# Attention followed by two MLPs on one core: short attention matmul runs held back until a second one is ready

## The chip, the cores and the metric

One core of a Trainium2 chip runs the whole program. The metric is the device time of one execution in microseconds (us), as the median of several executions. The engines are TensorE (PE in the profile; PEld is its weight load), VectorE (DVE), ScalarE (ACT), GpSimd (POOL) and SyncE (SP), which issues every DMA.

## The reference

```python
def _attn_ref(q, k, v):                      # (4, 8, 576, 64)
    out_d = sm_attn(q_d, k_d, v_d)           # q, k, v averaged over 4 positions: 144
    out_up = np.repeat(out_d, factor, axis=2)
    mask = np.abs(pos[:, None] - pos[None, :]) < factor
    scores = np.where(mask, scale * np.matmul(q, k.transpose(0, 1, 3, 2)), -1e9)
    ...
    return out_up + np.matmul(attn, v)
def _moe_ref(x, w_in, w_out):                # 2304 x 512, 512 x 2048, 2048 x 512
    g = np.maximum(x @ w_in, 0.0) ** 2
    return g @ w_out
def reference(...):                          # attention, then two such MLPs
```

The attention of a batch is the sum of a coarse part (all heads over 144 averaged positions) and a local part (a band of seven positions around the diagonal). Its result, 2304 tokens of 512 numbers, goes through two MLPs of the same shape.

## The kernel before, in words

The MLPs work on nine tiles of 256 tokens. For each tile and each of eight slices p of the hidden layer, `mm_h` (L787) does 24 matmuls of 128 x 128 by 128 x 256, ACT squares the relu, and `mm_y` (L864) does 24 more. Weights and activations are split into a high part (wH, xH, gH) and a low part (xL, gL), each product being done in three. The first two tiles are interleaved slice by slice, since the weights are still being unpacked from 64 bits on ACT, DVE and POOL (L639, L641, L644, L653) in that time. I call these matmuls **F**: tiles 0 and 1 take F 1 to 768, and tile 2 begins at F 769.

The attention runs between them on TensorE, in short runs:

- `pool_qk` (three transposes, L383) and `pool_v` (POOL adds, L357 and L361, into vd) average q, k and v;
- `heads_of`, four times a batch: scores (L406), softmax, transposes of the probabilities (L433), product with the averaged values vd (L444), evacuation by ACT into outd;
- `group`, five times a batch, for 116 positions: transposes of q and k (L508), mask (L523) and scores (L532), softmax, transposes (L561), product with v (L579), and the sum with outd into the token tile xr (DVE, L591). ACT and POOL then split xr into xH (L329) and xL (L765) for the MLP.

The order of all of this is not written out. Each piece of work is a generator that yields what it needs next as an engine and an estimated duration; `Order.run` (L127 on) takes, again and again, the piece that could start earliest by its own estimate of time, and the instructions are issued in that order. So the order of all engines is fixed when the kernel is built, and each engine then runs its own list in sequence. The accumulators for the attention are whole PSUM tiles: at0 (at_138 in some listings), at1 and y. Once the MLP has begun, y and then at1 are given up to the MLP, so that until tile 1 has left, every attention run writes to at0 and waits until its last reader has finished.

`Order.fill` issues matmuls of no use while TensorE would be idle before the MLP begins (L990); it is unset at the MLP's first step.

Of the kernel before, what the change touches and what calls it, by code (L numbers as in the profile page):

```python
# [28 lines left out]
SAME = 0.03  # L29
TO_PE = 0.1  # L30
WINDOW = 10.24 / 3
COLS = 3300
NXL = 2
NXR = 2
# [7 lines left out]
NEAR = 0.02  # L42
# [7 lines left out]
class Thread:  # L50
    def __init__(self, gen, prio):
        self.gen, self.prio, self.ready, self.wish = gen, prio, 0.0, None
        self.last, self.done = None, 0.0


class Order:


    def __init__(self):
        self.free = {}  # L60
        self.columns = {}
        self.fill = None
        self.lanes = []
        self.live = []
        self.ev = {}

    def lane(self, width, todo):

        self.lanes.append((width, [Thread(g, p) for p, g in todo], []))
# [34 lines left out]
    def slow(self, t):  # L104

        return self.columns.get(int(t / WINDOW + 1e-9) - 1, 0.0) < COLS

    def stream(self, t, dur, rows=1.0):

        while dur > 1e-6:  # L110
            w = int(t / WINDOW + 1e-9)
            rate = 0.5 if self.slow(t) else 1.0
            part = min(dur, ((w + 1) * WINDOW - t) * rate)
            self.columns[w] = self.columns.get(w, 0.0) + part * 2400 * rows
            dur -= part
            t += part / rate
        return t

    def start(self, th, eng):
        own = 0.0 if eng == th.last == "SP" else th.done  # L120
        if eng != th.last:
            own += LATENCY.get(th.last, 0.0)
        elif eng not in ("PE", "SP"):
            own += SAME
        t = max(th.ready, own) + (TO_PE if eng == "PE" and th.last != "PE" else 0.0)
        t = max(t, self.free.get(eng, 0.0))
        return max(t, self.free.get("DMA", 0.0) - AHEAD) if eng == "SP" else t  # L127

    def run(self):
        while True:  # L130
            self.poll()
            best = None
            for th in self.live:
                if th.wish is not None and not callable(th.wish):
                    some = th.wish if isinstance(th.wish, list) else [th.wish]
                    _, t, eng, dur, *rows = min((self.start(th, w[0]) + w[1] * BIAS.get(w[0], 1.0), self.start(th, w[0]), *w) for w in some)
                    key = t
                    if best is None or key < best[0] - NEAR:
                        best = key, t, th, eng, dur, rows
            if best is None:  # L140
                assert not self.live, "nothing can start"
                return
            _, t, th, eng, dur, rows = best
            self.eng = eng
            if eng == "PE":
                if self.fill:
                    now = max(self.free.get("PE", 0.0), FT)
                    while now + FG < t:
                        now = self.stream(now, 0.22, 1.0)
                        self.fill()  # L150
                dur = self.stream(t, dur, *rows) - t
            if eng == "SP":
                self.free[eng] = t + (rows[0] if rows else 0.46)
                self.free["DMA"] = max(t + 1.1, self.free.get("DMA", 0.0)) + dur
                value = self.free["DMA"] + 2.0
            else:
                self.free[eng] = t + dur
                value = t + dur + LATENCY[eng]
            th.last, th.done = eng, value - LATENCY[eng]
            self.resume(th, value)  # L160
# [46 lines left out]
def attention_two_mlp_kernel(  # L207
# [101 lines left out]
    def dve(cols):  # L309
        return "DVE", 0.165 + cols / 960.0  # L310

    def dve2(cols):

        return "DVE", 0.2 + cols / 720.0
# [4 lines left out]
    def pool(cols):  # L319
        return "POOL", 0.12 + cols * 0.0026  # L320

    def act(cols):
        return "ACT", 0.185 + cols / 1200.0

    def engine():
        return nc.vector if o.eng == "DVE" else nc.gpsimd

    def evac(dst, src):
        nc.scalar.activation(out=dst, in_=src, func=AF.Copy)  # L329
# [5 lines left out]
    def count(key, n, t):  # L335

        c = counts.setdefault(key, [0, 0.0])
        c[0] += 1
        c[1] = max(c[1], t)
        if c[0] == n:  # L340
            ev[key] = c[1]
        return c[0] == n
# [51 lines left out]
    def heads_of(b, hp):  # L394

        yield o.at("pooled", b)
        m = yield from f_hd.take()
        pp, nm, sm = hd_[m], nm_[m][:, 0], nm_[m][:, 1]
        p4 = pp.rearrange("p (c g) -> p c g", c=4)
        a = yield from f_at.take()  # L400
        s = pair[a][0:72, :, 0:288].rearrange("p j (a g) -> p j a g", a=2)
        tt = yield "PE", 0.4
        for qh in range(2):
            for j in range(2):
                js = slice(64 * j, 64 * j + 64)
                nc.tensor.matmul(  # L406
                    out=s[:, j, qh], lhsT=qd[js, hp, 72 * qh:72 * qh + 72], rhs=kd[js, hp], start=True, stop=True
                )
        count(("scored", b), 4, tt)
        yield dve(576)  # L410
        nc.vector.tensor_reduce(out=nm.rearrange("p (j a) -> p j a", j=2), in_=s, op=ALU.max, axis=AX.X)
        yield "DVE", 0.2
        nc.vector.tensor_scalar_mul(nm, nm, -1.0 / 128.0)
        for c in range(4):
            tt = yield "ACT", 0.57
            nc.scalar.activation(
                out=p4[:, c], in_=s[:, c // 2, c % 2], func=AF.Exp, bias=nm[:, c:c + 1], scale=1.0 / 128.0,
                accum_out=sm[:, c:c + 1],
            )
        f_at.put(a, tt)  # L420
        yield "DVE", 0.2
        nc.vector.tensor_scalar(out=sm, in0=sm, scalar1=1e-9, scalar2=4.0, op0=ALU.add, op1=ALU.mult)
        yield "DVE", 0.2
        nc.vector.reciprocal(out=sm, in_=sm)
        yield [dve2(576), pool(576)]
        engine().tensor_tensor(out=p4, in0=p4, in1=sm.unsqueeze(2).to_broadcast([72, 4, GD]), op=ALU.mult)
        a = yield from f_at.take()
        yield "PE", 0.55, 0.56
        for j in range(2):
            for kh in range(2):  # L430
                for qh in range(2):
                    c = kh * 144 + qh * 72
                    nc.tensor.transpose(  # L433
                        pair[a][0:72, j, c:c + 72], p4[:, 2 * j + qh, kh * 72:kh * 72 + 72], ident[0:72, 0:72]
                    )
        yield act(576)
        evac(pp.rearrange("p (j c) -> p j c", j=2), pair[a][0:72, :, 0:288])
        yield o.at("vpooled", b)
        if b > 1:
            yield o.at("local", b - 2)  # L440
        tt = yield "PE", 0.5
        for kh in range(2):
            for j in range(2):
                nc.tensor.matmul(  # L444
                    out=pair[a][64 * j:64 * j + 64, 0, 288:432], lhsT=vd[:, 4 * j + hp, kh],
                    rhs=pp[:, j * 288 + kh * 144:j * 288 + kh * 144 + 144], start=(kh == 0), stop=(kh == 1),
                    skip_group_check=True,
                )
        count(("pved", b), 4, tt)
        tt = yield act(288)  # L450
        evac(
            outd[b % 2][:, 2 * (hp % 2) + hp // 2].rearrange("p (g r) -> p g r", r=2),
            pair[a][:, 0, 288:432].unsqueeze(2).to_broadcast([128, GD, 2]),
        )
        f_at.put(a, tt)
        f_hd.put(m, tt)
        count(("heads", b), 4, tt)
# [30 lines left out]
    def group(b, i):  # L488
# [16 lines left out]
        tt = yield "PE", 0.9  # L505
# [6 lines left out]
        tt = yield act(1024)  # L512
# [4 lines left out]
        u = yield from f_pb.take(b == 0)  # L517
        p, nm, sm = pb_[u], nmb_[u][:, 0], nmb_[u][:, 1]
        a = yield from f_at.take()
        yield "PE", 0.4  # L520
        mask = mask16[0 if i == 0 else 2 if i == NG - 1 else 1]
        for j in range(2):
            nc.tensor.matmul(  # L523
# [3 lines left out]
        tt = yield "PE", 0.5  # L527
# [15 lines left out]
        tt = yield dve(512)  # L543
# [18 lines left out]
        tt = yield act(512)  # L562
# [6 lines left out]
        t0, t1 = (b * S + q0) // TN, (b * S + q0 + nq - 1) // TN  # L569
        yield from x_tiles(t0, t1)  # L570
        a = yield from f_at.take()
        tt = yield "PE", 0.6
        xp = pair[a].rearrange("p j (i c) -> p (j i) c", i=2)
        for i2 in range(2):
            for c, qa, nb, w0 in blocks:
# [9 lines left out]
        for c, qa, nb, w0 in blocks:  # L585
            g = b * S + qa
            for t in range(g // TN, (g + nb - 1) // TN + 1):
                c0, c1 = max(g, t * TN), min(g + nb, t * TN + TN)
                o0, g0, n2 = 64 * c + c0 - g, (c0 - b * S) // 2, (c1 - c0) // 2
                tt = yield dve(4 * (c1 - c0))  # L590
# [369 lines left out]
    for b in range(B):  # L960
        t = b * S / TN - 2
        heads += [(t + QP, pool_qk(b, s_, d_, c)) for c in range(3) for s_, d_ in ((q, qd), (k, kd))]
        heads += [(t + VP, pool_v(b, kh, j)) for kh in range(2) for j in range(2)]
        heads += [(t + HP, heads_of(b, hp)) for hp in range(4)]
        vees += [((b * S + GQ * i) / TN + UP, values(b, i)) for i in range(NG)]
        groups += [((b * S + GQ * i) / TN + GP, group(b, i)) for i in range(NG)]
# [78 lines left out]
```

## Time and profile before

| what | us |
|---|---|
| median of three executions | 973.45 |
| lowest, highest | 972.92, 977.17 |
| profiled execution | 971.34 |
| its span, first to last instruction | 969.6 |
| TensorE busy in it | 930.5 (96%) |

TensorE is busy nearly all of the time from about 100 us on, and the attention's last run is over by about 408 us. The span is 1.7 us shorter than the time of its own execution, and that execution is 2.1 us below the median. "Idle before" in a row is time in which the engine stood still, and what stands behind the arrow is what ended it. The granted clock is given as a share of 2.4 GHz.

### The profile page before, as it was taken

What the parts mean: (1) busy time and instruction counts of PE and PEld (TensorE: products, weight loads), DVE (VectorE), ACT (ScalarE), POOL (GpSimd) and SP (SyncE); (2) the same over time, 40 slices, a digit from 0 to 9 for tenths busy, and PEclk for the clock granted to TensorE, in tenths of its full rate; (3) what the DMA queues carried; (4) which work ended last, traced back from release to release, by engine and by line L of the source; (5) the groups of instructions that cost most, each with busy time, mean ns of one, the idle gap of its engine ahead of it and who ended that gap; (6) DMA issues with size and microseconds to landing.
All of it is one profiled execution on the core that took longest, in us unless ns stands there. A gap on an engine that the chain in (4) does not pass through costs nothing.

```text
span 969.6 us, 21378 instructions
## 1 busy us (share of the span) xinstructions
PE 930.5 (96%) x8795; PEld 889.2 (92%) x8795; DVE 502.3 (52%) x1016; ACT 515.4 (53%) x1044; POOL 250.9 (26%) x236
## 2 busy tenths in 40 slices
PE   7877999999999999999999999999999999999996
PEld 4457888999999999999999999999999999999996
DVE  5599796333353666655311226545454554545454
ACT  4466666455565565544443656545455554545543
POOL 5265563236134200101653454201010110101000
PEclk9798999999999999999999999999999999999999
DMA  9676565146147466675230544011010101100000
GB/s 237 151 209 191 168 177 131 43 136 163 48 119 196 142 208 212 213 242 182 67 102 30 172 134 150 3 45 44 2 44 2 45 1 45 45 1 23 1 23 23
DMA packets 99538, 101.00 MB, mean 104 GB/s; under 512 B 66672, under 2 KB 72304, under 8 KB 99440
## 3 DMA queue, kind: packets, MB, share of 16 engines
q1 hardware_dynamic: 99440, 99.64, 34.8%
q8 instruction: 69, 1.13, 0.5%
q14 instruction: 29, 0.24, 0.1%
HBM read 80.74 MB, written 18.87 MB: 103 GB/s over the span
## 4 chain that ended last, share of the span: by engine, by line
PE 84%; DVE 6%; DMA 3%; ACT 3%; POOL 2%; issue 1%; SPq 1%; DVEq 0%; POOLq 0%; ACTq 0%
PE h L787 39%; PE y L864 17%; PE at L847 13%; PE y L847 5%; DVE ga L644 2%; PE at L864 2%; DMA ld<-in_moe_w_in_dram 2%; PE at L508 2%; PE at L532 1%; PE at L579 1%; DMA ld<-in_v_dram 1%; PE at L406 1%; PE h L990 1%; PE at L383 1%; PE at L561 1%
## 5 line engine op out<-in xcount | busy, mean ns | idle before, releaser
L787 PE MATMUL h<-xH,w 128*128 128x256 f32 x2304 | 325.1, 283 | 0.0
L787 PEld LDWEIGHTS h<-xH,w 128*128 128x128 f32 x2304 | 294.5, 190 | 2.2 <-issue 1.2
L796 ACT ACTIVATE h<-h 128x512 f32<-128x512 f32 x144 | 83.8, 582 | 199.6 <-PE h L787 199.5
L787 PE MATMUL h<-xL,w 128*128 128x256 f32 x1152 | 182.9, 280 | 0.0
L832 DVE TENSOR_TENSOR gL<-h,gH 128x512 fp32r<-128x512 f32 x144 | 98.6, 684 | 137.7 <-ACT gH L805 120.2
L787 PEld LDWEIGHTS h<-xL,w 128*128 128x128 f32 x1152 | 156.6, 189 | 0.0
L864 PE MATMUL y<-gH,w 128*128 128x256 f32 x1024 | 133.5, 283 | 2.9 <-ACT gH L805 2.9
L765 POOL TENSOR_TENSOR xL<-xr,xH 128x512 fp32r<-128x512 f32 x33 | 43.6, 1337 | 341.1 <-ACT xH L329 341.0
L828 DVE TENSOR_TENSOR S<-h,S 128x128 f32<-128x128 f32 x144 | 42.0, 291 | 169.5 <-ACT gH L805 165.3
L864 PEld LDWEIGHTS y<-gH,w 128*128 128x128 f32 x1024 | 125.6, 190 | 4.3 <-ACT gH L805 3.3
L644 DVE SCALAR_TENSOR_TENSOR ga<-ld,ga 128x512 int32<-128x512 int32 x128 | 109.4, 861 | 2.7
L811 ACT CAST SH<-S 128x512 fp32r<-128x512 f32 x72 | 44.7, 621 | 89.3 <-DVE S L828 89.3
L798 ACT ACTIVATE h<-h 128x512 f32<-128x512 f32 x144 | 84.1, 584 | 3.6
L805 ACT CAST gH<-h 128x512 fp32r<-128x512 f32 x144 | 84.6, 588 | 1.8 <-DVE S L828 0.5
L864 PE MATMUL y<-gL,w 128*128 128x256 f32 x512 | 72.1, 282 | 0.0
L864 PEld LDWEIGHTS y<-gL,w 128*128 128x128 f32 x512 | 64.4, 188 | 1.3 <-issue 1.0
L836 DVE TENSOR_TENSOR gSL<-S,SH 128x512 fp32r<-128x512 f32 x72 | 54.3, 755 | 9.2
L639 ACT ACTIVATE ga<-ld 128x512 f32<-128x512 f32 x64 | 42.9, 674 | 24.0 <-DMA ld<-in_moe_w_in_dram 12.8
L847 PE MATMUL at<-w,SH 128*128 128x256 f32 x224 | 45.6, 285 | 2.1 <-ACT SH L811 2.1
L653 POOL TENSOR_TENSOR w<-ga,w 128x512 fp32r<-128x512 f32 x23 | 32.8, 1428 | 48.1 <-ACT w L329 48.0
L641 DVE TENSOR_SCALAR ga<-ga 128x512 int32<-128x512 int32 x64 | 33.1, 517 | 23.4 <-ACT ga L639 23.4
L828 DVE TENSOR_TENSOR S<-S,h 128x128 f32<-128x128 f32 x144 | 41.4, 287 | 5.3 <-ACT gH L805 0.7
(271 smaller groups left out, 1402.2 us busy)
## 6 DMA issues: line engine op xcount, KB each, us to landing
ld<-in_moe_w_out_dram SPq DMA_DIRECT2D x32, 512.0 KB, 5.6
ld<-ws SPq DMA_DIRECT2D x24, 512.0 KB, 3.2
ld<-in_moe_w_in_dram SPq DMA_DIRECT2D x32, 256.0 KB, 3.7
ld<-in_moe_w_in_dram SPq DMA_DIRECT2D x16, 512.0 KB, 4.9
ws<-ga SPq DMA_DIRECT2D x32, 256.0 KB, 3.4
ys<-ld SPq DMA_DIRECT2D x9, 512.0 KB, 4.7
xr<-ys SPq DMA_DIRECT2D x9, 512.0 KB, 4.8
out_dram<-ld SPq DMA_DIRECT2D x9, 512.0 KB, 2.8
```

The source lines that it names most:

```text
L644: nc.vector.scalar_tensor_tensor(out=gi, in0=w32[:, :, word], scalar=amount, in1=gi, op0=op0, op1=ALU.bitwise_or)
L765: engine().tensor_tensor(out=xL[n % NXL][:, ks], in0=xr[i][:, ks], in1=xH[n % NXL][:, ks].bitcast(F32), op=ALU.subtract)
L787: nc.tensor.matmul(out=o, lhsT=w[:, kk, fs], rhs=x[:, kk], start=(i == 0), stop=(i == len(mms) - 1))
L796: nc.scalar.activation(out=h, in_=h, func=AF.Relu)
L798: nc.scalar.activation(out=h, in_=h, func=AF.Square)
L805: nc.scalar.copy(gH[i % 2], h)
L811: nc.scalar.copy(late2["SH"], late2["S"])
L828: nc.vector.tensor_tensor(out=dst, in0=a, in1=b, op=op)
L832: nc.vector.tensor_tensor(out=gL[i % 2], in0=h, in1=gH[i % 2].bitcast(F32), op=ALU.subtract)
L836: nc.vector.tensor_tensor(out=gSL, in0=late2["S"], in1=late2["SH"].bitcast(F32), op=ALU.subtract)
L847: nc.tensor.matmul(out=seven(n, m - 1), lhsT=lhsT, rhs=quarter(p, w, low), start=p == 0 and x == 0 and m not in (2, 3, 6), stop=p == NP - ...
L864: nc.tensor.matmul(out=yb[e // 2][:, (e % 2) * 256:(e % 2) * 256 + 256], lhsT=w[:, fi, e * 128:e * 128 + 128], rhs=g[:, fi * 256:fi * 256 ...
```

## The change

Five kinds of attention runs on TensorE get a fourth field, "parts", in what they yield: the coarse scores (L406), their transposes (L433), their product with the values (L444), the mask together with the local scores (L523; the scores L532 follow without a mark), and the local product (L579). For such a run the new `hold` may add to the time by which the next piece is chosen. Nothing is added while the filling matmuls are on, when the last thing on TensorE was itself such a run, or when a second marked run could start at the same time. Otherwise the run counts as ready only 2.5 us after its own last step was done. No instruction is added or removed; only the order changes. In the changed file the lines from `heads_of` on stand 11 further down (L444 is L455, L787 is L798, L864 is L875).

```diff
@@ -29,6 +29,7 @@
 WINDOW = 10.24 / 3
+HOLD = 2.5
 COLS = 3300
@@ -63,6 +64,7 @@
         self.ev = {}
+        self.parts = False
 
@@ -116,6 +118,14 @@
+    def hold(self, th, t):
+
+        if isinstance(th.wish, list) or len(th.wish) < 4 or self.parts or self.fill:
+            return 0.0
+        if sum(type(x.wish) is tuple and len(x.wish) > 3 and self.start(x, "PE") <= t + NEAR for x in self.live) > 1:
+            return 0.0
+        return max(0.0, th.done + HOLD - t)
+
@@ -134,7 +144,7 @@
-                    key = t
+                    key = t + self.hold(th, t)
                     if best is None or key < best[0] - NEAR:
@@ -143,12 +153,13 @@
             if eng == "PE":
+                self.parts = len(rows) > 1
                 if self.fill:
...
-                dur = self.stream(t, dur, *rows) - t
+                dur = self.stream(t, dur, *rows[:1]) - t
@@ -399,7 +410,7 @@
-        tt = yield "PE", 0.4
+        tt = yield "PE", 0.4, 1.0, "parts"
@@ -425,7 +436,7 @@
-        yield "PE", 0.55, 0.56
+        yield "PE", 0.55, 0.56, "parts"
@@ -438,7 +449,7 @@
-        tt = yield "PE", 0.5
+        tt = yield "PE", 0.5, 1.0, "parts"
@@ -517,7 +528,7 @@
-        yield "PE", 0.4
+        yield "PE", 0.4, 1.0, "parts"
@@ -569,7 +580,7 @@
-        tt = yield "PE", 0.6
+        tt = yield "PE", 0.6, 1.0, "parts"
```

Three places in the lists of instructions, each before and with the change, show what moves.

TensorE where token tile 2 begins (pb0, pb1: probabilities of the first two groups of batch 1; h0 with xH0 is tile 2), before:

```order
L561 MATMUL at0_138<-ident_63,pb1_90 128x128 x4
L864 MATMUL at1_139<-gH0_70,w610_1597 128x256 x4
L864 MATMUL at1_139<-gH0_70,w611_1598 128x256 x4
L864 MATMUL at1_139<-gH0_70,w610_1597 128x256 x4
L864 MATMUL at1_139<-gH0_70,w611_1598 128x256 x4
L579 MATMUL at0_138<-pb1_90,vw1_88 64x58 x16
L864 MATMUL at1_139<-gL0_72,w610_1597 128x256 x8
L864 MATMUL at1_139<-gH1_71,w710_1760 128x256 x4
L864 MATMUL at1_139<-gH1_71,w711_1761 128x256 x4
L864 MATMUL at1_139<-gH1_71,w710_1760 128x256 x4
L864 MATMUL at1_139<-gH1_71,w711_1761 128x256 x4
L508 MATMUL at0_138<-ident_63,ld3_82 128x128 x8
```

and with the change:

```order
L572 MATMUL at0_138<-ident_63,pb0_89 128x128 x4
L875 MATMUL at1_139<-gL1_73,w710_1716 128x256 x8
L590 MATMUL at0_138<-pb0_89,vw0_87 64x58 x16
L572 MATMUL at0_138<-ident_63,pb1_90 128x128 x4
L590 MATMUL at0_138<-pb1_90,vw1_88 64x58 x16
L519 MATMUL at0_138<-ident_63,ld0_79 128x128 x8
L798 MATMUL h0_141<-xH0_68,w000_137 128x256
L798 MATMUL h0_141<-xH0_68,w001_136 128x256
```

Before, 16 MLP matmuls stand between the second group's transposes and its product, and 24 between that and the transposes of the third group; eight more, a mask and a score run follow before tile 2 begins. Now the first group's product, the second group's two steps and the third group's transposes follow one another with nothing between, all in at0, and tile 2 begins right behind them.

POOL in the time of batch 1's coarse part (vd: averaged values; w: low halves of weights; hd: probabilities), before:

```order
L653 TENSOR_TENSOR w401_120<-ga0_83,w400_121 128x512
L357 TENSOR_TENSOR ld3_82<-ld3_82 72x4x128
L361 TENSOR_TENSOR vd_99<-ld3_82 72x4x64
L653 TENSOR_TENSOR w411_118<-ga0_83,w410_119 128x512
L653 TENSOR_TENSOR w411_118<-ga1_84,w410_119 128x512
L357 TENSOR_TENSOR ld1_80<-ld1_80 72x4x128
L361 TENSOR_TENSOR vd_99<-ld1_80 72x4x64
L653 TENSOR_TENSOR w501_116<-ga0_83,w500_117 128x512
L426 TENSOR_TENSOR hd0_102<-hd0_102,nm0_104 72x576
L357 TENSOR_TENSOR ld0_79<-ld0_79 72x4x128
L361 TENSOR_TENSOR vd_99<-ld0_79 72x4x64
L653 TENSOR_TENSOR w511_1410<-ga0_83,w510_115 128x512
```

and with the change:

```order
L368 TENSOR_TENSOR ld2_81<-ld2_81 72x4x128
L372 TENSOR_TENSOR vd_99<-ld2_81 72x4x64
L664 TENSOR_TENSOR w311_122<-ga1_84,w310_123 128x512
L664 TENSOR_TENSOR w401_120<-ga0_83,w400_121 128x512
L368 TENSOR_TENSOR ld2_81<-ld2_81 72x4x128
L372 TENSOR_TENSOR vd_99<-ld2_81 72x4x64
L664 TENSOR_TENSOR w401_120<-ga1_84,w400_121 128x512
L437 TENSOR_TENSOR hd0_102<-hd0_102,nm0_104 72x576
L368 TENSOR_TENSOR ld2_81<-ld2_81 72x4x128
L368 TENSOR_TENSOR ld3_82<-ld3_82 72x4x128
L372 TENSOR_TENSOR vd_99<-ld2_81 72x4x64
L372 TENSOR_TENSOR vd_99<-ld3_82 72x4x64
```

The four pairs of adds that make vd now all stand ahead of the low half of weight block w501, which is POOL's next row. Before, two pairs stand ahead of it, the third behind it, and the fourth below these rows, behind w511. On SP the fourth load for them follows eleven loads of weight blocks instead of sixteen, counted from the first place at which the lists differ.

TensorE at the first product of batch 1's coarse part, with the change:

```order
L875 MATMUL y<-gH_70,w_118 128x256 x4
L455 MATMUL at_138<-hd_102,vd 64x144 x4
L875 MATMUL y<-gL_72,w_119 128x256 x8
L444 MATMUL at_138<-ident,hd_103 72x72 x8
L798 MATMUL h_141<-xH_68,w_117 128x256
```

Here the transposes of the second pair of heads (L444, before L433) come eight MLP matmuls after the first product (L455, before L444). Before, 20 stand between them. The product now comes after 352 F (before 400), the transposes ahead of it after 304 (before 360), and the second score run, whose place in at0 they take, after 256 (before 288). The third transposes stand after 544 (before 552), 64 F behind the fourth scores instead of 36.

## Rows read from the trace of the kernel before

**Rows 1.** Head of the page: the span.

```profile
span 969.6 us, 21378 instructions
```

**Rows 2.** Busy us by stretch of PE, PEld, DVE, ACT, POOL; then clock.

```profile
66.00:110.00 44.00, 34.33 (x281) 31.81 (x280) 37.36 (x52) 26.72 (x49) 24.59 (x19) 0.82 0.67 195
110.00:200.00 90.00, 85.91 (x834) 81.84 (x833) 57.59 (x91) 52.78 (x115) 37.73 (x30) 0.98 0.45 119
200.00:410.00 210.00, 209.40 (x2504) 197.79 (x2504) 110.57 (x220) 120.53 (x260) 58.26 (x59) 1.00 0.56 162
```

**Rows 3.** Waits of TensorE, 62 to 170 us: total us, times, longest.

```profile
PE at L561 <- POOL e L557: 3.2, 1, 3.2
PE y L864 <- ACT gH L805: 2.9, 1, 2.9
PE at L383 <- POOL ld L377: 2.7, 2, 1.8
PE at L433 <- issue: 1.6, 1, 1.6
PE at L444 <- POOL vd L361: 1.5, 1, 1.5
```

**Rows 4.** Chain of waits, undisturbed MLP matmuls: start us, us.

```profile
446.40 2.83 PE y L864 x24
```

**Rows 5.** Order of time: a score run alone (start, us).

```profile
156.02 1.10 PE L787 MATMUL h<-xH,w 128*128 128x256 f32 x8
...
157.52 0.71 PE L406 MATMUL at<-kd,qd 64*72 64x144 f32 x8
158.17 1.21 PE L787 MATMUL h<-xH,w 128*128 128x256 f32 x8
...
159.68 2.04 PE L864 MATMUL y<-gH,w 128*128 128x256 f32 x16
```

**Rows 6.** Order of time: a value run and a score run together.

```profile
248.29 2.13 PE L864 MATMUL y<-gH,w 128*128 128x256 f32 x16
250.35 0.71 PE L444 MATMUL at<-hd,vd 72*64 72x144 f32 x8
251.64 1.21 PE L864 MATMUL y<-gL,w 128*128 128x256 f32 x8
252.78 0.71 PE L406 MATMUL at<-kd,qd 64*72 64x144 f32 x8
```

**Rows 7.** Busy us by stretch around the wait at L444.

```profile
136.50:139.90 3.40, 1.87 (x16) 1.29 (x14) 3.37 (x4) 1.70 (x3) 3.21 (x3) 1.00 0.66 186
139.90:143.30 3.40, 3.40 (x17) 3.38 (x17) 2.06 (x2) 1.99 (x4) 2.11 (x2) 0.50 0.64 202
```

**Rows 8.** Order of time: L444 after that wait, [idle before], and its evacuation.

```profile
139.54 0.46 PE L444 MATMUL at<-hd,vd 72*64 72x144 f32 x2 [1.53 <-POOL vd L361]
...
142.31 0.41 ACT L329 ACTIVATE outd<-at 128x288 f32<-128x288 f32 x1
```

**Rows 9.** Order of time: batch 1's second scores and first transposes.

```profile
121.78 0.71 PE L406 MATMUL at<-kd,qd 64*72 64x144 f32 x8
...
131.94 0.67 PE L433 MATMUL at<-ident,hd 72*72 72x72 f32 x8 [0.78 <-ACT hd L416]
```

**Rows 10.** Order of time: a group's last steps up to tile 2.

```profile
191.82 0.60 PE L561 MATMUL at<-ident,pb 128*128 128x128 f32 x4
...
192.51 0.59 ACT L329 ACTIVATE pb<-at 128x512 f32<-128x512 f32 x1
...
194.17 0.69 PE L579 MATMUL at<-pb,vw 64*64 64x58 f32 x32
...
194.95 0.77 DVE L591 TENSOR_TENSOR xr<-at,outd 128x232 f32<-128x232 f32 x3
195.52 1.15 ACT L329 ACTIVATE xH<-xr 128x512 fp32r<-128x512 f32 x2 [1.31 <-DVE xr L591]
196.23 2.52 POOL L765 TENSOR_TENSOR xL<-xr,xH 128x512 fp32r<-128x512 f32 x2 [7.67 <-ACT xH L329]
```

## The prediction

> **What bounds the kernel now.** I read the head of the page first, then busy time by stretch, then who waited for whom, and last the order of time at the places that the change moves. The span is 969.6 us [rows 1]. By stretch [rows 2], TensorE stands still for 44.0 - 34.3 = 9.7 us between 66 and 110 us, for 90.0 - 85.9 = 4.1 us up to 200, and for only 0.6 us from there to 410, where the attention has just ended. The reader should see that the attention is no load of its own any more after 200 us: TensorE runs on without a gap, so the end comes when its list is through. Time can be won or lost only in two ways: what TensorE itself spends on its list, and the waits and low clock of the first 200 us. Those waits are on single steps [rows 3]: transposes waiting for POOL (L561, L383), an MLP step waiting for ACT (L864), transposes of batch 1 (L433), and the first product of batch 1 that waits for the averaged values (L444). DVE is busy 37.4 of 44 us in the first stretch [rows 2]; it unpacks weights there and passes its lateness on to ACT and POOL.
>
> **The change, part by part.** The profiled execution took 971.34 us; I add to that, and carry the difference over to the median of 973.45, which is 2.1 us higher.
>
> *Fewer switches.* 24 MLP matmuls take 2.83 us, 0.118 each [rows 4]. A score run alone [rows 5]: the twelve ahead of it take 157.52 - 156.02 = 1.50 instead of 1.41, the run 0.65, and the twelve behind it 1.51 instead of 1.41, so 0.65 of work and 0.19 for going in and out, 0.84 together. A product and a score run next to each other [rows 6] take 1.29, with about 0.08 ahead and 0.10 behind: 1.47, where two alone at that price would take 1.68. Joining two runs is thus worth up to 0.2 us. In the list of TensorE the MLP matmuls are cut into 84 pieces before and 79 with the change, and the groups of marked runs fall from 72 to 67. Five joins are worth 0 to 1.0 us; I take 0.12 each, as some joins have whole-array transposes or masks in them: **-0.6**.
>
> The Trainium skill, TensorEngine Tiling, section Key Properties, says that TensorE drains when the tiling mode changes, and not when only the tile does. By that rule a join of two runs cut in different ways, as a product (72 x 64) and a score run (64 x 72) are, would still drain once between them, and five joins would save about half of the two passages each, some 0.5 us. The rows show no step between them that is longer than the way out, so the rule speaks against a large gain and agrees with the size that I take.
>
> *The wait for the averaged values.* On POOL the four pairs of adds now stand ahead of w501, and the product comes after 352 F instead of 400. Their loads stand earlier on SP by five loads of weight blocks. DVE's instructions take 37.36 / 52 = 0.72 us each in the first stretch [rows 2], and a block has at least three of them (L641 and L644 twice): 2.2 us, so that five blocks are some 11 us. The product is 48 x 0.118 = 5.7 us earlier, and with the old wait of 1.5 it needs 7.2. So the values come first, and the wait of 1.5 us goes [rows 3]. After that wait the granted clock stood at 0.50, 1.2 GHz, for 3.4 us [rows 7], which cost 1.7 us; the stretch before it had TensorE at work for 1.87 of 3.4 us. Both together: **-3.2** (bounds: 0 and -3.2). The weight blocks that fall behind those adds come later on POOL; no MLP matmul waited for a weight there [rows 3], and were that cover too thin, it would eat this term first.
>
> *Third transposes of batch 1.* They come 64 F after the fourth scores instead of 36, 28 x 0.118 = 3.3 us more room, for a wait of 1.6 [rows 3]: **-1.6** (0 to -1.6).
>
> *Second transposes.* These stand eight F (0.9 us) behind the first product and write the same PSUM tile at0, which must be evacuated by ACT first. In the trace the product's last matmuls start at 139.54, and the evacuation ends at 142.72 [rows 8]: about 2.8 us after the product's end, because other work is ahead on ACT. If that stays, the wait is 1.9 us; if ACT comes at once, none. I take the middle: **+1.0**.
>
> *First transposes.* They follow the second scores by 48 F (5.7 us) instead of 72. From those scores to the transposes it took 10.2 us, of which 0.8 was TensorE's wait [rows 9]. At the same pace the wait would be 3.6; DVE's two steps on these scores (L411, L413) now follow one another, though, where weight work stood between them, and that takes about 2 us out. I take 1.7 instead of 0.8: **+0.9** (-0.8 to +2.8).
>
> *The start of tile 2.* This is the largest term. Now the last steps of two groups follow each other in at0. From transposes to the end of their evacuation it takes 193.10 - 191.82 = 1.28 us, from a product to the end of its sums 195.72 - 194.17 = 1.55, and from a product to the end of xL 198.75 - 194.17 = 4.58 [rows 10]. The new chain is 1.28 + 1.55 + 1.28 + 4.58 and two last matmuls, 8.9 us. TensorE has in that time two runs of transposes (0.35 each to the next start), two products (0.62 and 0.2 for going in and out), eight transposes (0.8) and 20 F (2.4): 5.5 us. It stands still for 3.4 us, where before nearly nothing was lost; nothing can cover it, since the MLP matmuls of tile 2 are next on TensorE's list and wait themselves. The clock may fall too: of the two waits of about 1.5 us above, at L444 and L433, one was followed by a slow stretch and one was not, so I add half of 1.7. **+4.25** (bounds: 0, if TensorE is late anyway, and 3.4 + 3.4 with two slow stretches).
>
> *No term.* The waits between 66 and 110 us are left as they are: TensorE's order moves there (24 F instead of 12 ahead of the first mask), but its waits end with POOL and ACT work that hangs on DVE's list, which keeps its weight work. Where one comes sooner, the next one takes it up. After 200 us TensorE's cover is long, and waits of a microsecond or less may come and go.
>
> Sum: -0.6 - 3.2 - 1.6 + 1.0 + 0.9 + 4.25 = +0.75, or 972.1 us for an execution like the profiled one and **974.2 us** for the median.
>
> **The rivals.** *Faster: the first stretch moves as well.* TensorE waits there 3.2 us for L561's input and 2.9 for L864's [rows 3], and the clock is 0.82 over the stretch [rows 2]. With the change, 12 F stand between L561 and the product, and POOL takes one half of xL and one subtraction that DVE had. If these two waits and two slow stretches (1.7 each) go altogether, that is -9.5; if two thirds of that, -6.3, and the time is 967.9. Against it: L561 hangs on POOL work behind DVE, whose list is as long up to there. It decides when more than 5.6 us come out, the bound of "faster" being 4.9 below the median. *Slower: one PSUM tile for all.* The marked runs stand closer, and until tile 1 has left they share at0. If the two transposes' waits come at their upper ends (1.9 and +2.8 instead of 1.0 and 0.9, so +2.8) and the start of tile 2 has two slow stretches (+2.55), the time is 974.2 + 5.4 = 979.6. It decides when these waits exceed the gains by 4.9. *Nothing to speak of:* only five of 72 groups are joined, and if moved waits cancel, -0.6 is left: 972.9.
>
> **How the numbers follow.** My own forecast, that a gain before tile 2 is spent at its start, has a chance of 0.36, the rival without effect 0.13; both lie within 0.5% (4.9 us, about what a measurement of this kernel can tell from no change). Faster has 0.27, since twice the net sum is at stake in the first stretch, and slower 0.24. The range reaches from 967.5 to 980.0, through both rivals' times; outside of it are the full loss of the first waits below, and both upper ends with a lost gain above.
>
> **What would show it.** In the new profile: no wait of L455 for POOL and no half clock behind it; waits of the transposes (now L444) for ACT; at the start of tile 2 four short waits one after another, on ACT, DVE and POOL, of 3 to 4 us in all; about 79 pieces of MLP work. I am wrong if the start of tile 2 shows no stall, if the waits from 66 to 110 us change by more than 3 us in sum, or if waits above 1 us appear after 210 us.

## The result: slower by 11 us, and the profile after

The changed kernel takes 984.41 us (median of four executions, 983.52 to 986.76), the kernel before, run beside it, 973.18 us (970.49 to 977.17). The ratio is 1.012 [1.009, 1.015]. The forecast was 974.2 us with a range up to 980.0, so the result lies outside of it. The profiled execution took 983.52 us, 12.2 us more than that of before.

The page's head and busy time by stretch, to be held against [rows 1, 2] (columns as there; the last row is a stretch that I had not read before predicting, and the same stretch of the kernel before is below it):

```profile
span 981.6 us, 21351 instructions
```

```profile
66.00:110.00 44.00, 33.36 (x278) 31.09 (x278) 38.30 (x51) 26.57 (x48) 28.11 (x22) 0.80 0.64 189
110.00:200.00 90.00, 84.80 (x794) 81.23 (x793) 59.15 (x87) 51.32 (x112) 34.03 (x27) 0.96 0.44 123
200.00:410.00 210.00, 208.19 (x2484) 196.40 (x2485) 103.38 (x210) 119.88 (x256) 59.99 (x60) 0.99 0.51 145
410.00:570.00 160.00, 155.32 (x1330) 154.65 (x1329) 61.22 (x96) 74.57 (x138) 46.22 (x50) 0.98 0.44 145
```

```profile
410.00:570.00 160.00, 160.00 (x1367) 159.73 (x1366) 48.77 (x75) 77.03 (x140) 58.06 (x61) 1.00 0.40 133
```

In each of the first three stretches TensorE is busy for about one microsecond less. In the fourth, where the attention is long over, it stands still for 4.7 us and is at a lower clock, where before it ran without a gap. The lists differ in a little more than their order: the planner also moved eight of the element-wise steps that DVE and POOL share from POOL to DVE. TensorE's waits, from 62 to 170 us (against [rows 3]), from 170 to 410, and from 410 to 600:

```profile
PE y L875 <- ACT gH L816: 4.4, 1, 4.4
PE at L394 <- POOL ld L388: 4.2, 3, 3.0
PE at L444 <- ACT hd L427: 3.4, 1, 3.4
PE at L519 <- DVE w L664: 3.4, 1, 3.4
PE at L572 <- POOL e L568: 2.1, 1, 2.1
PE at L444 <- POOL w L664: 0.9, 1, 0.9
```

```profile
PE at L572 <- DVE xr L602: 1.0, 1, 1.0
PE at L519 <- DVE xr L602: 1.0, 1, 1.0
PE at L590 <- ACT pb L340: 0.7, 1, 0.7
```

```profile
PE y L875 <- ACT ld L943: 4.7, 1, 4.7
```

The wait of the product for the averaged values (L455, L444 before) is gone, as forecast, and three short waits are at tile 2's start. The 3.4 us at L519 are not new; the same transposes waited before, for a load, which [rows 3] leave out:

```profile
PE at L508 <- DMA e<-in_q_dram: 2.9, 1, 2.9
```

New are 3.4 us at the first transposes of batch 1 (L444 for L427), and 4.7 us for ACT's copies of a finished tile (`leave`, L943).

**Where the time went.** Since all kernels here issue the same MLP matmuls in nearly the same places, I count F in the trace and take the time between the k-th ones. F 552 is near the end of batch 1's coarse part, tile 2 begins behind F 768, the attention ends before F 2303, tile 7 begins behind F 2688, and layer 2 behind F 3456. This table has one profiled execution of each kernel, in us; the runs in it come further down. What follows F 4000 takes 326.7 to 328.5 us in all of them.

```
                 to F 0  0-264 264-552 552-2303 2303-2688 2688-3000 3000-3456 3456-4000
before             66.0   52.8    45.8    275.8      45.5      36.7      53.7      66.5
after              66.5   53.8    46.1    278.6      45.5      44.2      53.7      66.5
e3_hold_early      66.0   52.9    46.3    281.8      44.0      36.7      53.7      66.5
e4_hold_late       66.1   54.8    45.7    279.3      44.0      43.2      60.4      66.8
e5_after_fix       65.8   53.9    46.3    279.9      45.5      36.7      53.7      68.9
e6_before_fix      67.4   51.1    46.6    275.8      45.5      36.7      53.7      67.0
e7_late_fix        64.0   55.5    46.1    277.2      44.0      36.7      53.7      73.1
e8_hold_0p5        65.4   53.0    46.4    274.4      45.5      43.0      53.7      66.5
e9_first_only      67.0   53.4    48.6    276.7      45.5      36.7      53.8      66.2
e10_tile2_only     63.8   53.1    44.9    277.6      45.5      36.7      53.7      68.5
e11_hold_0p5_fix   66.1   53.5    46.1    275.2      44.0      36.7      53.7      69.0
```

After minus before: +0.5, +1.0, +0.3, +2.8, 0, **+7.5**, 0, 0. The largest piece, three fifths of the loss, falls at one place behind F 2688. Here is the order of time there, in the changed kernel (start, us, [idle before]):

```profile
490.47 1.10 PE L798 MATMUL h<-xH,w 128*128 128x256 f32 x8
...
493.50 0.58 ACT L807 ACTIVATE h<-h 128x512 f32<-128x512 f32 x1 [6.01 <-PE h L798]
...
496.32 0.58 ACT L807 ACTIVATE h<-h 128x512 f32<-128x512 f32 x1 [1.01 <-PE h L798]
...
498.20 0.43 ACT L340 ACTIVATE q_outd<-ld 128x256 fp32r<-128x256 f32 x1
...
499.44 0.41 ACT L340 ACTIVATE q_xr<-ld 128x256 fp32r<-128x256 f32 x1
499.74 1.17 ACT L943 COPY ld<-y 128x512 f32<-128x512 f32 x2
500.96 1.44 PE L875 MATMUL y<-gH,w 128*128 128x256 f32 x5 [4.68 <-ACT ld L943]
```

and in the kernel before:

```profile
485.96 1.10 PE L787 MATMUL h<-xH,w 128*128 128x256 f32 x8
486.15 1.07 ACT L932 COPY ld<-y 128x512 f32<-128x512 f32 x2 [1.33 <-PE y L864]
```

At 490.47 TensorE begins tile 7; tile 6 is complete in y. Before, ACT copies y out at once. In the changed kernel ACT has nothing to do for 6.0 us, but its next row is the relu of tile 7's first slice; the copies stand behind the relus of two slices and six casts of quarter weights (`q_outd`, `q_vd`, `q_xr`, made in `quarters`). These are needed only by the second MLP: it does its second product not as 24 matmuls a slice but as 21, by seven block products (`mm_y2`) that work on quarters of the weight block and on differences of them. After those two slices the first `mm_y` of tile 7 is next on TensorE; it writes y and must wait for the copies. The order of ACT's list, not its load, sets the end here.

Why the copies came to stand there: `leave` takes one of the load buffers ld. When the attention is over and the second MLP's weights are unpacked, `make_room` gives up ld2 and ld3, and two lanes of `quarters` take ld0 and ld1 in turn. With the change this begins later: the attention's last sum starts at 412.4 us instead of 407.9, the last step of that unpacking on DVE at 467.7 instead of 455.0, and the first cast of quarter weights on ACT at 480.9 instead of 465.1. The unpacking moved by more than the attention, and in the run e8 below by itself (461.9 us, with the attention's last sum at 405.9); why the planner put it off is not shown. At the moment when tile 6 was done in the planner's own time, both buffers were with the quarter weights, so that it got one two slices later. In ACT's list of before, tile 6's copies stand behind 56 relu pairs (seven tiles of eight slices) and 12 casts of quarter weights, after the change behind 58 and the same 12; before, those casts had been done while tile 6 was still at work.

### The profile page after: what moved, and what is told of

It reads as the page before. It is cut to its first block, busy times and chain, and to the rows that moved or that the text cites. A ratio compares the mean times of both kernels' runs of the same rounds, so it can differ in the third digit from the quotient of the medians.

```text
span 981.6 us, 21351 instructions
## 1 busy us (share of the span) xinstructions
PE 933.2 (95%) x8795; PEld 892.4 (91%) x8795; DVE 509.1 (52%) x1024; ACT 517.1 (53%) x1044; POOL 248.3 (25%) x228
## 4 chain that ended last, share of the span: by engine, by line
PE 84%; DVE 7%; ACT 4%; DMA 2%; issue 2%; POOL 2%; SPq 0%; DVEq 0%; ACTq 0%; POOLq 0%
PE h L798 38%; PE y L875 17%; PE at L858 13%; PE y L858 5%; DVE ga L655 3%; PE at L875 2%; PE at L519 2%; PE h L1001 1%; PE at L543 1%; PE at L590 1%; DVE ga L652 1%; PE at L455 1%; PE at L572 1%; PE at L444 1%; DMA ld<-in_moe_w_in_dram 1%
## 5 line engine op out<-in xcount | busy, mean ns | idle before, releaser
L798 PE MATMUL h<-xH,w 128*128 128x256 f32 x2304 | 324.2, 283 | 0.0
L798 PEld LDWEIGHTS h<-xH,w 128*128 128x128 f32 x2304 | 294.7, 190 | 1.4 <-issue 1.0
L798 PE MATMUL h<-xL,w 128*128 128x256 f32 x1152 | 183.1, 280 | 0.0
L798 PEld LDWEIGHTS h<-xL,w 128*128 128x128 f32 x1152 | 156.8, 189 | 0.0
L875 PE MATMUL y<-gH,w 128*128 128x256 f32 x1024 | 135.1, 285 | 9.1 <-ACT ld L943 4.7
L875 PEld LDWEIGHTS y<-gH,w 128*128 128x128 f32 x1024 | 127.0, 191 | 10.6 <-ACT ld L943 4.9
L655 DVE SCALAR_TENSOR_TENSOR ga<-ld,ga 128x512 int32<-128x512 int32 x128 | 105.0, 822 | 3.0
L875 PE MATMUL y<-gL,w 128*128 128x256 f32 x512 | 74.3, 288 | 0.0
L875 PEld LDWEIGHTS y<-gL,w 128*128 128x128 f32 x512 | 66.5, 194 | 1.4 <-issue 0.8
L652 DVE TENSOR_SCALAR ga<-ga 128x512 int32<-128x512 int32 x64 | 36.0, 562 | 23.0 <-ACT ga L650 22.9
```

What stands on the lines that cost most here:

```text
L652: nc.vector.tensor_single_scalar(out=gi, in_=gi, scalar=3, op=ALU.logical_shift_left)
L655: nc.vector.scalar_tensor_tensor(out=gi, in0=w32[:, :, word], scalar=amount, in1=gi, op0=op0, op1=ALU.bitwise_or)
L798: nc.tensor.matmul(out=o, lhsT=w[:, kk, fs], rhs=x[:, kk], start=(i == 0), stop=(i == len(mms) - 1))
L875: nc.tensor.matmul(out=yb[e // 2][:, (e % 2) * 256:(e % 2) * 256 + 256], lhsT=w[:, fi, e * 128:e * 128 + 128], rhs=g[:, fi * 256:fi * 256 ...
```

## The experiments

The ratios are to the kernel before, run beside each (medians 973.8 us for e1 to e4, 973.58 for e5 to e8, 972.86 for e9 to e11). Theory A was at first: the piece at 496 us is the order of ACT that the quarter weights bring about, and the rest is the early part; the rivals are in the expectations. Lines of a run can stand up to four further down than in the changed kernel (L877 for L875, L945 for L943).

**One lane for the quarter weights**, in the changed kernel (e1) and in the kernel before (e2). With one lane instead of two, T1 of some slices (a difference that `quarters` writes back to where these weights are loaded from) is formed only after the second MLP's weights are loaded anew, so both compute the second MLP with other numbers; the work is the same in kind and amount.

```diff
-    o.lane(2, [(98, quarters(0)), (98, quarters(1))])
+    o.lane(1, [(98, quarters(0)), (98, quarters(1))])
```

> The changed kernel with one lane for the quarter weights of the second MLP instead of two. TensorE's list stays as in the changed kernel; on ACT the evacuation of tile 6's result moves from behind 58 relus to behind 56. Theory A (of the 11 us lost, 7.4 are TensorE's wait for that evacuation at 496 us and the low clock behind it, 4.5 are lost by the end of the attention): 976.5 to 978.5 us, no wait of L875 for L943 after 410 us. Rival B (the time after the attention is lost for another reason, such as the weights' loads): 982 to 986.

> The kernel before with the same single lane: a control. Theory A: tile 6's evacuation stands behind 56 relus in both, so 972 to 975 us. If one lane by itself makes the quarter weights late or early, it shows here, as more than 2 us either way.

Measured: e1 1006.36 us, ratio 1.033 [1.029, 1.037]; e2 980.6 us, 1.007 [1.004, 1.010]. The wait at tile 6 is gone in e1, with F 3000 3.5 us after that of before instead of 11.9, but both totals are far above what A expected (976.5 to 978.5 and 972 to 975 us) and say nothing about it: with one lane the quarter weights come too late for layer 2. The wait that took the place, in e1:

```profile
PE at L858 <- ACT q_xr L340: 20.6, 1, 20.6
```

The missing wait at tile 6 is what A expected; the edit was too blunt to give the size.

**Holding only at first** (e3) and **only later** (e4), split at the moment tile 1 has left PSUM. In `hold`, as e3 has it (e4 has `not in`):

```diff
+        if ("left", 1) in self.ev:
+            return 0.0
         return max(0.0, th.done + HOLD - t)
```

> The changed kernel, with runs held only until tile 1 has left. TensorE's list is that of the changed kernel up to 768 F and another one after; tile 6's evacuation stands behind 56 relus. Theory A: the stall at the start of tile 2 (about 5 us on TensorE and the clock) is there, the wait at 496 us is not: 975 to 980 us. Rival B: 982 to 986.

> The changed kernel, with runs held only after tile 1 has left. TensorE's list is that of the kernel before up to 900 F, so nothing is lost before 220 us; the groups of marked runs are 67 as in the changed kernel. But tile 6's evacuation stands behind 58 relus and tile 7's behind 66. Theory A: one or two waits of about 5 us for L943 with low clock behind them, 979 to 988 us. Rival B (what is lost is lost where runs are held in one PSUM tile): 971 to 974.

Measured: e3 979.07 us, 1.005 [1.003, 1.008]; e4 986.11 us, 1.012 [1.007, 1.016], both within A's ranges. In e3 tile 6's copies stand behind 56 relu pairs, and F 2688 to 3000 takes 36.7 us as before; its profile is 6.5 us late at F 2303 and 6.9 at the end, so its loss is in the early part. In e4, whose TensorE list is that of before beyond tile 2's start, the copies of tile 6 and of tile 7 both come two slices late, and each costs some 6.6 us in the table:

```profile
PE y L877 <- ACT ld L945: 7.8, 2, 4.3
```

So each of the two pieces occurs without the other, and the late one follows the place of the copies in ACT's list, in both directions.

**Giving tile 6 its buffer first**, and nothing else: the lane that forms quarter group 3 waits until tile 6 has left, in the changed kernel (e5) and in the kernel before (e6). TensorE's list does not move by one instruction.

```diff
         for p in range(p0, NP, 2):
+            if p == 3:
+                yield o.at("left", 6)
             n = yield from f_ld.take()
```

> The changed kernel, with one added wait in the planner: the lane of the quarter weights that forms group 3 takes its load buffer only after tile 6 has left PSUM. TensorE's list stays the same, instruction for instruction; on ScalarE tile 6's two copies then stand behind 56 relu pairs and 2 groups of quarter casts instead of 58 and 4. Theory A (7.4 of the 11 us are the collision of tile 6's copies with the quarter weights in ScalarE's order): no wait of the first layer-1 matmul of tile 7 on those copies at 496 us, the 3000th MLP matmul 4.5 us after that of the kernel before instead of 11.9, and 975.5 to 979 us in all. Rival B (the loss at 496 us only shows there what TensorE already owed; without that wait another takes its place): 982 to 986 us. Rival C (the quarter weights, now later, hold up the start of layer 2, as in the runs with one lane): the 4000th MLP matmul is more than 3 us later against the 3456th than in the kernel before, 980 us or more.

> Control: the same added wait in the kernel before, where nothing waited at that place. TensorE's list is the same as before's. Theory A and rival B: 972 to 975 us, no difference; rival C: 976 us or more, from waits at the start of layer 2.

Measured: e5 979.52 us, 1.0055 [1.0035, 1.0075], 4.9 us below the changed kernel; e6 975.19 us, 1.0005 [0.998, 1.003], no difference that can be told from none. In e5 the copies now follow tile 6's last product at once:

```profile
491.57 1.07 ACT L945 COPY ld<-y 128x512 f32<-128x512 f32 x2 [3.19 <-PE y L877]
```

```profile
PE at L860 <- DVE gSL L849: 3.6, 3, 1.7
```

F 2688 to 3000 takes 36.7 us again: the whole 7.5 us is gone, and rival B falls. The second row is what is late next, at the start of layer 2, where F 3456 to 4000 takes 2.4 us more, because the quarter weights were put off: 7.5 less 2.4 is 5.1, against 4.9 in the medians. My range (975.5 to 979) left that out, and rival C held in part.

**Late holding with both tiles let out first** (e7). The quarter weights of the last groups are formed only after the second MLP's weights are loaded anew here, so that MLP is computed with other numbers.

```diff
+            if p in (wait := {1: 6, 6: 7}):
+                yield o.at("left", wait[p])
```

> The run that holds only after tile 1 has left, with two added waits in the planner for the quarter weights: group 1 takes its load buffer only after tile 6 has left, group 6 only after tile 7 has. TensorE's list is that of the run without the two waits. Theory A: the two waits of 7.8 us with their two slow stretches go, some 13 of the 17.5 us that its profile was longer; 971 to 976 us. If the holding costs something by itself after tile 1: 977 to 980. Rival B: 984 us or more.

Measured: 980.03 us, 1.004 [1.003, 1.006]: above what A expected. Both waits are gone (36.7 and 53.7 us in the table), but layer 2's start takes 6.6 us more. Up to F 2688 the profile is 0.8 us behind that of before, so holding after tile 1 costs nothing by itself that one profile could show.

**A short hold** (e8): `HOLD = 0.5`, with no other edit. TensorE's list is that of before up to row 637, just short of tile 2, but ACT's list has tile 6's copies behind 58 relu pairs again.

> HOLD = 0.5 instead of 2.5, nothing else: TensorE's list is the kernel before's up to row 637, so the first tiles are as before, and few runs are joined. But ScalarE's list again has tile 6's copies behind 58 relu pairs and all 12 quarter casts of the first groups. Theory A (the order at tile 6 costs by itself, whatever the holding does): a wait of 3 to 6 us on those copies near 490 us and 977 to 983 us. Rival D (the time follows the holding: little is held, little is lost): 971 to 975 us and no such wait.

Measured: 979.25 us, 1.005 [1.002, 1.008]. This is the run that tells A from the rival most plainly: with little held, it is 1.3 us ahead of before at F 2688, and then loses 6.3 us at the same place as the changed kernel:

```profile
493.03 0.41 ACT L340 ACTIVATE q_outd<-ld 128x256 fp32r<-128x256 f32 x1
...
493.95 1.17 ACT L943 COPY ld<-y 128x512 f32<-128x512 f32 x2
495.17 2.08 PE L875 MATMUL y<-gH,w 128*128 128x256 f32 x8 [4.68 <-ACT ld L943]
```

**The early part taken apart.** e9 holds only until the fourth slice of tile 1 and again once tile 1 has left; e10 holds only from the seventh slice of tile 1 on, and has e5's wait for group 3. The condition of e9, then that of e10:

```diff
+        if ("h", 1, 3) in self.ev and ("left", 1) not in self.ev:
+        if ("h", 1, 6) not in self.ev:
+            return 0.0
```

> The changed kernel, with no holding from the fourth slice of tile 1 until tile 1 has left. TensorE's list is the changed kernel's up to row 520, through the first three transposes of batch 1; then the products come earlier, the second group's product after 760 F instead of 768, with 8 F, a mask, a score run and transposes between it and tile 2. ScalarE's list has tile 6's copies behind 56 relu pairs and 6 quarter casts, as before. My account now: the transposes' wait for ScalarE at the first transposes stays (3 to 4 us, with half clock near 130 us), so the 552nd MLP matmul comes 1 to 2 us later than before; tile 2's first matmul waits 1 to 2 us instead of 2.7 in three waits with half clock behind; no wait at tile 6. 974.5 to 978 us. Rival (the first stretch costs nothing, all of the 4.5 us by the end of the attention is tile 2's start): the 552nd within 0.5 us of before, and 973 to 975. Rival (the loss is elsewhere in the attention): 979 or more.

> The changed kernel, with no holding until the seventh slice of tile 1, and with the added wait that lets tile 6 leave ahead of quarter group 3. TensorE's list is the kernel before's up to row 614, through everything of batch 1's coarse part; then the second group's product is held from 736 F to 768 F, with only one run of transposes between it and tile 2's first matmul. By [rows 10] the chain from that product to the end of xL takes 4.6 us, of which the product and the transposes cover 1.7: 2.9 us of waits at tile 2's start, and 0 to 1.7 us of slow clock. The added wait costs 0.4 to 2.5 us at the start of layer 2, as in the two runs with it. My account: 976.5 to 980 us, no wait of over 1 us at tile 6, and no first transposes waiting 3 us or more. Rival (tile 2's start was late anyway and costs nothing): 973 to 975.5.

Measured: e9 976.17 us, 1.003 [1.001, 1.005]; e10 978.56 us, 1.006 [1.003, 1.009]. Both are within their ranges. e9 keeps the late first transposes (4.8 us of wait) and loses 2.8 us between F 264 and 552, more than the 1 to 2 expected; from there to F 2303 it loses 0.9. e10 has before's coarse part, loses nothing up to F 552, and waits at tile 2:

```profile
PE at L521 <- DVE xr L604: 1.0, 1, 1.0
PE h L802 <- POOL xL L780: 0.7, 1, 0.7
PE at L521 <- ACT ld L947: 0.6, 1, 0.6
```

That is 2.3 us of waits where 2.9 were expected, and its stretch from F 552 to 2303 is 1.8 us longer than before's. Its profile is of its shortest execution (972.37 us, others up to 982.60), in which no slow stretch followed these waits; the median has more than the profile can show.

**Short hold and tile 6 first** (e11), e8 with e5's wait, as the version that the runs pointed to.

> HOLD = 0.5 as in the run before, with the added wait that lets tile 6 leave ahead of quarter group 3. TensorE's list is that of HOLD = 0.5, which in its profile was 1.3 us ahead of the kernel before at the 2688th MLP matmul and lost 6.3 us at tile 6. My account: that loss goes, and the start of layer 2 costs 0.4 to 2.5 us: 972 to 975.5 us, about 5 us less than without the wait. Rival (the wait at tile 6 is replaced by another): 977 us or more.

Measured: 974.09 us, 1.0004 [0.998, 1.003]; expected, 972 to 975.5. The loss at tile 6 is gone (5.2 us less than e8 in the medians), 2.5 us come at layer 2's start, and the rest is the kernel before. No version beat the kernel before.

## Why the prediction was wrong, by its own steps

**The step that failed is "No term".** It says that after 200 us TensorE's cover is long and waits of a microsecond or less may come and go. It rested on [rows 2], which end at 410 us, and it looked only at how much work TensorE has, not at the order of the engines that it waits for. What the runs showed: 7.5 of the 12.2 us of the profiled execution are lost at 496 us, 86 us after that stretch, by the place of tile 6's copies in ACT's list (e5, e8). The prediction's own condition for being wrong, "waits above 1 us appear after 210 us", is what happened. The lists were there to be read: comparing ACT's list of both kernels for the place of each tile's copies would have shown 56 relu pairs ahead of tile 6's against 58; I compared lists only around the held runs. How much is held did not decide whether this loss comes: e3 and e9 hold and are spared, e8 holds little and has it. It depends on how the planner's order happens to fall.

**The wait for the averaged values, the third, second and first transposes** (-3.2, -1.6, +1.0, +0.9, together -2.9). The mechanism of the first was right: no wait of L455 for POOL. But the sum over F 264 to 552 is 45.8 us before and 46.1 after, +0.3. What was gained came back for the most part at one term, the first transposes. The second, put at +1.0, did not wait at all (139.08 us, eight MLP matmuls behind the product at 137.40), and the third still waited 0.9 us instead of 1.6, so that 0.7 of the 1.6 were gained. For the first I had taken 2 us out of the chain from scores to transposes because two steps on DVE now follow each other; the trace after shows what I had not looked for, that the first of them stands behind weight unpacking:

```profile
118.62 0.71 PE L417 MATMUL at<-kd,qd 64*72 64x144 f32 x8
...
123.94 1.22 DVE L655 SCALAR_TENSOR_TENSOR ga<-ld,ga 128x512 int32<-128x512 int32 x1
125.08 0.74 DVE L422 TENSOR_REDUCE nm<-at 72x4 f32<-72x576 f32 x1
...
128.37 1.14 PE L444 MATMUL at<-ident,hd 72*72 72x72 f32 x8 [3.39 <-ACT hd L427]
```

DVE takes up the scores 6.5 us after they began, where before it took 2.7, from 121.78 [rows 9] to:

```profile
124.50 0.72 DVE L411 TENSOR_REDUCE nm<-at 72x4 f32<-72x576 f32 x1
```

The chain is 9.75 us instead of 10.16 [rows 9], only 0.4 shorter, and the wait 3.4 instead of 0.8: close to the upper end that I gave (+2.8 on 0.8). The clock then stands at half for two stretches:

```profile
127.60:131.00 3.40, 2.63 (x16) 2.66 (x17) 2.89 (x6) 3.01 (x9) 1.14 (x1) 0.50 1.02 265
131.00:134.40 3.40, 3.40 (x18) 3.40 (x18) 3.33 (x7) 2.13 (x4) 0.16 (x1) 0.50 0.55 159
```

TensorE is busy in them for 6.03 us, of which half, 3.0, is lost. The slow stretch that I counted as saved, 1.7 us [rows 7], was thus replaced by these. All five kernels with the early hold (after, e3, e5, e9, and e1, which has its list too) take 23.3 to 25.2 us from F 264 to 400, the others 19.5 to 22.1, and most win it back by F 552.

**The start of tile 2** (+4.25, with switches -0.6): right in kind and about in size. The order of time shows the chain, one step waiting for the next in at0:

```profile
198.38 0.69 PE L590 MATMUL at<-pb,vw 64*64 64x58 f32 x32
199.23 0.71 DVE L602 TENSOR_TENSOR xr<-at,outd 128x232 f32<-128x232 f32 x2 [1.88 <-PE at L590]
200.08 0.63 PE L572 MATMUL at<-ident,pb 128*128 128x128 f32 x4 [1.02 <-DVE xr L602]
200.80 0.60 ACT L340 ACTIVATE pb<-at 128x512 f32<-128x512 f32 x1 [2.60 <-PE at L572]
201.45 0.69 PE L590 MATMUL at<-pb,vw 64*64 64x58 f32 x32 [0.74 <-ACT pb L340]
202.30 0.77 DVE L602 TENSOR_TENSOR xr<-at,outd 128x232 f32<-128x232 f32 x3 [2.36 <-PE at L590]
203.13 1.97 PE L519 MATMUL at<-ident,ld 128*128 128x128 f32 x8 [0.99 <-DVE xr L602]
```

Three waits of 2.7 us together instead of four of 3.4, and one slow stretch, in which TensorE was busy for 2.97 us, so 1.5 lost:

```profile
202.70:206.10 3.40, 2.97 (x14) 2.98 (x15) 0.37 (x3) 2.71 (x5) 2.51 (x2) 0.50 0.24 53
```

With fewer switches that would be +3.65 by the prediction; F 552 to 2303 took 2.8 us more, in e5, with the same list, 4.1, and in e3, whose list is the same up to tile 2, 6.0. In the profiles of e5 and e3 the same three waits were followed by 6.8 us at half clock.

**Fewer switches** (-0.6): not shown, but not refuted. From F 0 to F 2303 the MLP matmuls are in 84 pieces before and 79 after. If I leave out idle time of over 0.25 us at a stretch and count time at low clock at half, 351.4 us remain before and 349.6 after; with other limits for idle time the difference is 0.4 to 2.0 us. That has the sign of the forecast and about its size or more, but kernels with the same 84 pieces differ by 1.5 us in this sum (351.3 to 352.8). [rows 6] leave out the score run that they are about, between their second and third row:

```profile
250.99 0.71 PE L406 MATMUL at<-kd,qd 64*72 64x144 f32 x8
```

A product and a score run side by side cost in the new profile what they cost there, 1.29 us:

```profile
251.14 0.71 PE L417 MATMUL at<-kd,qd 64*72 64x144 f32 x8
251.79 0.71 PE L455 MATMUL at<-hd,vd 72*64 72x144 f32 x8
252.43 1.21 PE L798 MATMUL h<-xH,w 128*128 128x256 f32 x8
```

Each of the two takes 0.65 us to the next start, as a score run alone does before MLP matmuls [rows 5]. By the rule of the Trainium skill that I weighed (TensorEngine Tiling (Array Packing), Key Properties), such a pair drains between its two cuts as well. The trace agrees with it in that the step between the two is no shorter than the way out, 0.65 us in both cases; no run here isolates a drain.

**The first waits**, left at nothing: F 0 to 264 took 53.8 us against 52.8, while the other kernels take 51.1 to 55.5 there, so this is within the scatter. The rival "the first stretch moves" fell; the rival "one PSUM tile for all" was right on the first transposes (near the upper end) and on tile 2's start as e5 and e3 had it, and wrong on the second transposes. Its 979.6 us are what the changed kernel takes without the wait at tile 6 (e5, 979.52), but 2.4 us of that are the edit's own cost, so the match is in part luck.

What stays open is how the early loss divides. In the medians it is some 3.5 to 5 us: e3, which loses next to nothing after F 2303, is 5.3 us above before, and e5 less its own 2.4 is 3.5 above. e9 and e10 suggest that both early places cost something: each is clear of before in its median (3.3 and 5.7 us), but e9 also holds after tile 1, and e10 has the added wait, which cost 0.4 to 2.5 us elsewhere. The kernels whose TensorE lists are that of before up to F 900 (before, e4, e6, e7) take 154.5 to 160.0 us from F 0 to there in their single profiles, so that no part of 2 us can be told apart there.

## What to carry to other kernels

Where a planner fixes the lists of all engines, a change in one stage must be followed to the end of every list, above all to places where two users share few buffers: compare not only what moved near the edit but the place of each evacuation relative to the work of the next tile. A slack of many microseconds of TensorE work covers lateness, but not an evacuation that stands in its engine's list behind work which itself hangs on TensorE's next rows. And a reordering that joins runs should be priced first by the join: here a join was worth up to 0.2 us [rows 6], and each wait that came with the new order took 0.7 to 4.7.

## What the runs showed of the hardware that I had not expected

A wait can cost much more than its length, and the extra is not fixed by the wait. At 496 us TensorE waited 4.7 us, and then the granted clock stood at half, 1.2 GHz, until 506.5:

```profile
499.60:503.00 3.40, 2.04 (x9) 2.04 (x10) 1.31 (x3) 1.31 (x3) 0.69 (x1) 0.51 0.28 58
503.00:506.50 3.50, 3.50 (x19) 3.50 (x18) 0.00 (x0) 0.00 (x0) 1.15 (x2) 0.51 0.71 243
```

TensorE was busy for 5.54 us of them at 1.2 GHz, where 2.4 GHz would have taken half, 2.77; with the wait of 4.68 that makes the 7.5 us of the table. In e8 the same wait of 4.68 us was followed by only 3.4 us at half clock, and the place cost 6.3 us. At tile 2 the 2.3 us of waits in e10 were followed by no slow stretch, and the 2.7 us at the same place by 3.4 us at half clock in the changed kernel and by 6.8 in e5.
